# Keys as weights in a fused attention and cosine FFN kernel: scores with keys on partitions, and no turned exponentials

## The chip, the cores and the metric

The kernel runs on one core of one Trainium2 chip. The metric is the device time of one execution in microseconds, the median of several runs. The engines are TensorE (PE; its weight loads are shown apart as PEld), VectorE (DVE), ScalarE (ACT), GpSimd (POOL) and SyncE (SP), which issues the DMA transfers.

## The reference

```python
B, N, C = 4, 12480, 128;  n_agents = 49;  d_ff = 2048      # w_in, w_out float64, the rest float32
def sm(a, b):
    s = (a @ b.transpose(0, 2, 1)) / np.sqrt(128)
    s = s - s.max(-1, keepdims=True)
    e = np.exp(s)
    return e / (e.sum(-1, keepdims=True) + 1e-09)
agent_v = sm(agents, k) @ v        # 49 agents look at 12480 keys
x = (sm(q, agents) @ agent_v).reshape(B * N, 128)
h = x @ w_in                       # 49920 tokens, 2048 columns
out = (h * np.cos(h)) @ w_out
```

## The kernel before

**Main loop.** Each of the 4 batches has 13 groups of 960 queries, 52 groups q in all. A group takes 16 steps, two column halves c of 480 by eight steps i of 256 columns of d_ff, so there are 832 steps n. A step makes the first product on TensorE (`first_product`, L1011: two matmuls with the turned, normalized query weights pT as the moving operand, into one of three PSUM buffers `ph`), the cosine of it on ScalarE (L1014), r = (cos - 1) * h, called the cubic part, on VectorE (L1020), and four steps later (LAG) the second product on TensorE (L1036), which gathers in a PSUM buffer `one`; at the last step of a half two more matmuls (L1032, L1033) add what the -1 took away. `a` is agent_v times w_in, so that x is never made.

**Query weights.** For a group of queries TensorE makes scores (`query_scores`, L169: 32 matmuls with 30 queries as weights and 49 columns each, on four column tiles of TensorE), ScalarE or VectorE copies them to `e`, VectorE takes the maximum (L636), GpSimd subtracts it (L638; `query_both` makes two groups at once, L693), ScalarE takes exponentials of a piece of up to seven groups in one instruction (`query_exp`, L700), GpSimd sums (`query_sum`: additions in a tree, L711, and three small ones, L713 to L715) and, ten steps before the group is used, multiplies by the inverse (L724). `query_turned`, seven steps before, transposes on TensorE (L733), copies to `p` on ScalarE (L737), and on GpSimd makes for each half c a cast of one half of the rows of pT and a subtraction for the other (L740, L741). There are three pT buffers, q % 3; `first_product` of group q reads them.

**Keys of batches 1 to 3** (class `Later`; batch 0 is `First`, ahead of the loop). The work for batch b is done while the loop is at batch b - 1, whose 208 steps are one period. `scores` (13 groups of 1024 keys): two matmuls of 512 columns with the agents as weights, one into rows 0 to 63 and one into rows 64 to 112 of a buffer `one` (L524, L526), so that agents lie on partitions and keys in columns; ScalarE copies to `s` (L531), VectorE takes the maximum of the 512 (L532). `top` makes of these the shift of each agent. The first three groups of batch 1 are scored ahead of the rest, in a short window of their own near the start of the loop (`early_fill`). Then, 97 steps into the period, comes the burst: ScalarE loads its table of exponentials and takes, one after the other, seven groups of queries (A), all keys (L536, 113 x 6240, with the bias of the shift and a sum into `accum_out`) and the other six groups of queries (B). After it `turn` brings keys to partitions (four transposes L544, a copy L548 to `et`), and `values` multiplies them with the values (32 matmuls on four column tiles, L491) and adds to `av` on VectorE (L563). At the period's end `folded`, `inverse` (L501 to L503), `project` and `project_out` make the next batch's `a` and `b1`, `b2`.

**Order.** `Plan` lists, by step, the side work that is written between the loop's instructions; `extra` takes the next free step, `spread_out` spreads a list up to a step, `fill` puts side work into the five steps behind a burst, `mixed` merges two lists. The instructions are then ordered by a scheduler for each engine, by readiness. Fixed against it are what `keep_in_program_order` and `behind` name, the seven steps of a burst on TensorE, VectorE and ScalarE (`as_traced(queues[:3])`, so not GpSimd), side work on VectorE (`kept_behind`) and the late sums of piece B on GpSimd. Loads on SP are held 24 steps back (`load`). Everything else on GpSimd stands where the scheduler puts it, and each engine works through its queue in order.

## Time and profile before

| what | value |
|---|---|
| median of 3 runs | 1119.84 us (1119.44 to 1119.99) |
| the profiled execution: time, its span | 1121.91 us, 1120.1 us |
| mean granted clock of TensorE | 0.979 of full speed |
| TensorE busy | 1060.6 us (95%) |
| VectorE busy | 1028.8 us (92%) |
| ScalarE busy | 980.5 us (88%) |
| GpSimd busy | 373.2 us (33%) |
| chain that ended last | TensorE 62%, VectorE 25%, ScalarE 7% |

The shares are means over the whole span. The three bursts (near 230, 490 and 760 us) and the two stages around each of them, key scores before and values after, have limits of their own, and are read stretch by stretch. A row of the groups gives instructions of one line with their busy time, the mean of one, and the idle time of the engine before them with what ended most of it.

### The profile page before, as it was taken

How to read it: one execution, taken by the hardware profiler on the slowest of the kernel's cores; microseconds unless marked ns; L12 is line 12 of the kernel's file. 1: busy time of each engine (PE TensorE's matmuls, PEld its weight loads, DVE VectorE, ACT ScalarE, POOL GpSimd, SP SyncE). 2: the span in 40 equal slices, each digit the busy share in tenths (PEclk: the TensorE clock that was granted, in tenths of full speed). 3: DMA queues.
4: the chain of work that ended last, by engine and by line, in shares of the span. 5: the costliest groups of instructions: out<-in, count | busy, mean ns of one | idle time of the engine just before them, and what ended most of it. 6: DMA issues, size and time to landing. Idle time of an engine off the chain costs nothing.

```text
span 1120.1 us, 26308 instructions
## 1 busy us (share of the span) xinstructions
PE 1060.6 (95%) x10719; PEld 795.0 (71%) x10719; DVE 1028.8 (92%) x1156; ACT 980.5 (88%) x1275; POOL 373.2 (33%) x658
## 2 busy tenths in 40 slices
PE   6779999799999999989999999979999999989997
PEld 2666677588876776768887777658887777767774
DVE  5749999699999999989998999989999999999997
ACT  4758988888889999998888999999998999999996
POOL 2012322583222313286313232258331323162320
PEclk9889999899999999989999999989999999999999
DMA  9734445523102233434111233441300000000001
GB/s 360 268 129 129 129 145 202 184 94 110 61 19 85 72 120 127 149 128 131 59 56 37 75 107 111 150 147 57 106 28 19 36 18 36 36 18 36 18 36 38
DMA packets 32545, 108.31 MB, mean 97 GB/s; under 512 B 3616, under 2 KB 4896, under 8 KB 32416
## 3 DMA queue, kind: packets, MB, share of 16 engines
q1 hardware_dynamic: 32416, 106.55, 28.2%
q8 instruction: 86, 1.41, 0.5%
q14 instruction: 43, 0.35, 0.1%
HBM read 80.97 MB, written 25.56 MB: 95 GB/s over the span
## 4 chain that ended last, share of the span: by engine, by line
PE 62%; DVE 25%; ACT 7%; issue 3%; DMA 2%; SPq 0%; POOL 0%; ACTq 0%; DVEq 0%
PE ph L1011 24%; DVE r L1020 22%; PE one L1036 22%; ACT c L1014 3%; PE one L491 3%; PE one L169 2%; PE one L544 2%; ACT s L536 1%; PE one L1032 1%; PE one L1033 1%; DMA c<-qT 1%; PE one L733 1%; PE ph L491 1%; PE one L524 1%; PE one L374 1%
## 5 line engine op out<-in xcount | busy, mean ns | idle before, releaser
L1020 DVE SCALAR_TENSOR_TENSOR r<-c,ph 128x960 fp32r<-128x960 f32 x832 | 910.8, 1148 | 36.7 <-ACT c L1014 33.5
L1014 ACT ACTIVATE c<-ph 128x960 f32<-128x960 f32 x832 | 791.1, 980 | 88.0 <-PE ph L1011 66.4
L1011 PE MATMUL ph<-pT,a 113*128 113x480 f32 x1664 | 536.1, 402 | 10.3 <-DVE r L1020 7.2
L1036 PE MATMUL one<-r,w 128*128 128x480 f32 x1664 | 512.6, 391 | 2.6 <-ACT osb L1043 0.9
L1011 PEld LDWEIGHTS ph<-pT,a 113*128 113x128 f32 x1664 | 295.2, 190 | 137.6 <-DVE r L1020 77.3
L1036 PEld LDWEIGHTS one<-r,w 128*128 128x128 f32 x1664 | 309.4, 190 | 62.0 <-issue 8.1
L724 POOL TENSOR_TENSOR p<-e,rz 126x392 f32<-126x392 f32 x51 | 43.1, 846 | 288.3 <-PE one L733 265.4
L741 POOL TENSOR_TENSOR pT<-p,pT 49x480 fp32r<-49x480 f32 x102 | 124.4, 1219 | 7.8
L638 POOL TENSOR_TENSOR e<-e,mx 126x392 f32<-126x392 f32 x43 | 36.3, 844 | 231.5 <-DVE mx L636 231.5
L740 POOL CAST pT<-p 49x480 fp32r<-49x480 f32 x102 | 59.4, 583 | 83.8 <-ACT p L737 79.4
L1043 ACT COPY osb<-one 128x480 f32<-128x480 f32 x80 | 44.8, 560 | 2.3 <-PE one L1036 2.2
L169 PEld LDWEIGHTS one<-ag,xt 128*32 128x32 f32 (+1 forms) x2752 | 33.1, 109 | 17.9 <-issue 14.5
L711 POOL TENSOR_TENSOR tree<-tree 126x96 f32<-126x96 f32 x132 | 39.9, 302 | 9.9
L169 PE MATMUL one<-ag,xt 128*32 128x49 f32 (+1 forms) x2752 | 39.4, 209 | 3.0 <-issue 2.8
L524 PE MATMUL one<-xt,agp 128*64 128x512 f32 (+1 forms) x78 | 39.7, 591 | 1.7 <-DVE tops L528 1.7
L1032 PE MATMUL one<-pT,b 113*128 113x480 f32 x104 | 40.6, 391 | 0.0
L1033 PE MATMUL one<-pT,b 113*128 113x480 f32 x104 | 40.1, 386 | 0.0
L526 PE MATMUL one<-xt,agp 128*49 128x512 f32 (+1 forms) x78 | 39.2, 585 | 0.0
L491 PEld LDWEIGHTS one<-et,vt 128*32 128x32 f32 (+1 forms) x2352 | 28.4, 109 | 13.3 <-issue 11.0
L544 PE MATMUL one<-ident,s 113*128 113x113 f32 (+1 forms) x147 | 23.4, 284 | 13.5 <-ACT s L536 11.3
L491 PE MATMUL one<-et,vt 128*32 128x49 f32 (+1 forms) x2352 | 33.8, 208 | 0.0
L733 PEld LDWEIGHTS one<-ident,p 126*113 126x113 f32 x204 | 28.7, 176 | 4.4 <-POOL tree L711 0.5
(148 smaller groups left out, 670.5 us busy)
## 6 DMA issues: line engine op xcount, KB each, us to landing
outT<-osb SPq DMA_DIRECT2D x51, 480.0 KB, 2.6
xt<-qT SPq DMA_DIRECT2D x49, 480.0 KB, 3.7
xt<-kT SPq DMA_DIRECT2D x43, 512.0 KB, 3.7
vt<-vk SPq DMA_DIRECT2D x42, 512.0 KB, 4.3
c<-kT SPq DMA_DIRECT2D x5, 512.0 KB, 7.6
vt<-w_in SPq DMA_DIRECT2D x8, 256.0 KB, 7.7
vt<-w_out SPq DMA_DIRECT2D x8, 256.0 KB, 7.8
c<-vk SPq DMA_DIRECT2D x3, 512.0 KB, 7.8
```

Source lines behind the costliest of these rows:

```text
L169: mm = nc.tensor.matmul(out[at:at + n], xt[:, t * TT + lo:t * TT + lo + n], ag, start=True, stop=True)
L491: mm = nc.tensor.matmul(po[rows], vt[:, h * k + t, rows], e[:, t, h * HI:h * HI + NA], start=(first and t == h == 0), stop=(last and t == ...
L524: mm = nc.tensor.matmul(ps[:HI], agp[:, self.b], xt[:, :n], start=True, stop=True)
L544: mm = nc.tensor.transpose(pt[:, t], part[:, t * w:(t + 1) * w], ident[:KR, :KR])
L740: nc.gpsimd.tensor_copy(pT[own, c], p[own])
L741: nc.gpsimd.tensor_sub(pT[other, c], p[own], pT[own, c].bitcast(F32))
L1011: nc.tensor.matmul(ph[:, j, :CH], ai[:, f], pTs[q % 3][:, c], start=True, stop=True)
L1014: nc.scalar.activation(cos, h, AF.Sin, bias=HALF_PI, scale=1.0)
L1020: nc.vector.scalar_tensor_tensor(r, cos, 1.0, h, op0=ALU.subtract, op1=ALU.mult)
L1032: nc.tensor.matmul(po, b1[k], pTs[q % 3][:, c], start=False, stop=False)
L1033: nc.tensor.matmul(po, b2[k], pTs[q % 3][:, c], start=False, stop=False)
L1036: nc.tensor.matmul(po, w1[:, f, :], r[:, j, :], start=(f == 0), stop=(f == NF - 1))
```

## The change

For batches 1 to 3 the keys become the weights of their own scores: 32 matmuls on four column tiles for 1024 keys, as for queries, so that `s` is [128 keys, 98, 49 agents] and keys lie on partitions at once. The last group is 2 tiles of 96 keys; the empty rows are set to -1e30. Per group VectorE keeps a running maximum of 392 columns (`run`) where it reduced 512. `top`, `across` and `spread` (a reduction, a transpose with a reduction, a matmul that brings the maximum to all partitions) stand 22 steps before the burst, and 13 subtractions on GpSimd (`shift`) follow them, one a step; three groups of queries are scored after them. The exponential of the keys is one instruction of 4802 columns without bias and sum. The sum comes from 12 additions on GpSimd (`add`), planned 47 steps after the burst's start and every third step from there, and from a reduction, a copy and a matmul with ones at the period's end (`total`, `inverse`). `turn` is gone; `values` reads `s` itself, and the burst's third step gets two of them in the place of two turns.

```diff
@@ -404,6 +404,8 @@

     FULL = 2 * 4 * P
     NL = -(-N // FULL)
+    REST = (N - (NL - 1) * FULL) // 2
+    NT_K = 8 * (NL - 1) + 2
...
@@ -481,17 +484,15 @@
             self.av = self.sb.tile([P, KR], F32, name="av", bufs=2)
             nc.gpsimd.memset(self.av[:, NA:HI], 0.0)

-        def weighted(self, po, e, vt, first, last):
-
-            _, k, _ = e.shape
-            for t in range(k):
-                for h in range(2):
-                    for j in range(P // QS):
-                        rows = slice(j * QS, (j + 1) * QS)
-                        mm = nc.tensor.matmul(po[rows], vt[:, h * k + t, rows], e[:, t, h * HI:h * HI + NA],
-                                              start=(first and t == h == 0), stop=(last and t == k - 1 and h == 1))
-                        if t == h == j == 0:
-                            behind(mm)
+        def weighted(self, po, es, vt, first, last):
+
+            for x, e in enumerate(es):
+                for j in range(P // QS):
+                    rows = slice(j * QS, (j + 1) * QS)
+                    mm = nc.tensor.matmul(po[rows], vt[:, x, rows], e,
+                                          start=(first and x == 0), stop=(last and x + 1 == len(es)))
+                    if x == j == 0:
+                        behind(mm)
...
     class Later(First):

-
-
         def scores(self, g, by_vector=False):
             sb = self.sb
             if g == 0:
-                self.s = sb.tile([KR, N // 2], F32, name="s", bufs=1)
-                self.tops = sb.tile([KR, NL], F32, name="tops", bufs=1)
-                self.zs = sb.tile([KR, 1], F32, name="zs2", bufs=1)
-                self.turned = {}
-                self.m, self.z = (sb.tile([KR, 2], F32, name=x, bufs=1) for x in ("m", "z"))
-                for x in (self.m, self.z):
-                    nc.gpsimd.memset(x, 0.0)
+                self.s = sb.tile([P, NT_K, NA], F32, name="s", bufs=1)
+                self.run = sb.tile([P, 8, NA], F32, name="run", bufs=1)
+                self.es = sb.tile([P, 8, NA], F32, name="es", bufs=1)
+                nc.gpsimd.memset(self.s[REST:, 8 * (NL - 1):], -1e30)
             n = min(FULL, N - g * FULL)
             xt = sb.tile([P, 2 * 512], F32, name="xt", bufs=3)[:, :n]
             load(xt, kT[self.b, :, g * FULL:g * FULL + n])
-            n //= 2
-            ps = self.psum()[:KR, :n]
-            mm = nc.tensor.matmul(ps[:HI], agp[:, self.b], xt[:, :n], start=True, stop=True)
-            behind(mm)
-            nc.tensor.matmul(ps[HI:KR], agp[:, self.b, :NA], xt[:, n:], start=True, stop=True)
-            if by_vector:
-                nc.vector.tensor_tensor_reduce(self.part(g), ps, zero.to_broadcast([KR, n]), 1.0, LOWEST, op0=ALU.add,
-                                               op1=ALU.max, accum_out=self.tops[:, g:g + 1])
-            else:
-                nc.scalar.copy(self.part(g), ps)
-                nc.vector.reduce_max(self.tops[:, g:g + 1], ps, axis=AX.X)
-
-        def exp(self, g, n):
-            e = self.s[:, g * FULL // 2:min((g + n) * FULL, N) // 2]
-            return nc.scalar.activation(e, e, AF.Exp, bias=self.shift, scale=SC, accum_out=self.zs[:, :1])
-
-        def turn(self, g, by_vector=False):
-            part = self.part(g)
-            n = part.shape[-1]
-            k, w = -(-n // P), min(n, P)
-            pt = self.psum()[:w, :k * KR].rearrange("p (t a) -> p t a", a=KR)
+            s = self.part(g)
+            w, k, _ = s.shape
+            ps = self.psum()[:w, :k * NA].rearrange("p (t a) -> p t a", a=NA)
             for t in range(k):
-                mm = nc.tensor.transpose(pt[:, t], part[:, t * w:(t + 1) * w], ident[:KR, :KR])
-                if t == 0:
-                    behind(mm)
-            e = self.sb.tile([P, CH], F32, name="et", bufs=3)[:w, :k * KR].rearrange("p (t a) -> p t a", a=KR)
-            (nc.vector.tensor_copy if by_vector else nc.scalar.copy)(e, pt)
-            self.turned[g] = e
+                for j in range(w // QS):
+                    mm = nc.tensor.matmul(ps[j * QS:(j + 1) * QS, t], xt[:, t * w + j * QS:t * w + (j + 1) * QS],
+                                          ag[:, self.b, :], start=True, stop=True)
+                    if t == j == 0:
+                        behind(mm)
+            (nc.vector.tensor_copy if by_vector else nc.scalar.copy)(s, ps)
+            if g > 0:
+                run = self.run[:w, :k]
+                nc.vector.tensor_max(run, self.part(0) if g == 1 else run, s if by_vector else ps)
+
+        def part(self, g):
+            return self.s[:, 8 * g:8 * g + 8] if g + 1 < NL else self.s[:REST, 8 * g:]
+
+        def top(self):
+            self.m = self.sb.tile([P, NA], F32, name="m", bufs=1)
+            nc.vector.tensor_reduce(self.m, self.run.rearrange("p t a -> p a t"), axis=AX.X, op=ALU.max)
+
+        def across(self):
+            pt = self.psum()
+            nc.tensor.transpose(pt[:NA, :P], self.m, ident)
+            mx = self.sb.tile([NA, 1], F32, name="mx", bufs=1)
+            nc.vector.reduce_max(mx, pt[:NA, :P], axis=AX.X)
+            self.mxw = self.sb.tile([NA, P], F32, name="mxw", bufs=1)
+            nc.vector.tensor_copy(self.mxw, mx.to_broadcast([NA, P]))
+
+        def spread(self):
+            pb = self.psum()
+            nc.tensor.matmul(pb[:, :NA], self.mxw, ident[:NA, :NA], start=True, stop=True)
+            self.mxb = self.sb.tile([P, NA], F32, name="mxb", bufs=1)
+            nc.vector.tensor_copy(self.mxb, pb[:, :NA])
+
+        def shift(self, g):
+            s = self.s[:, 8 * g:min(8 * g + 8, NT_K)]
+            nc.gpsimd.tensor_sub(s, s, self.mxb.unsqueeze(1).to_broadcast(list(s.shape)))
+
+        def exp(self):
+            return nc.scalar.activation(self.s, self.s, AF.Exp, scale=SC)
+
+        def add(self, g):
+            s = self.s[:, 8 * g:min(8 * g + 8, NT_K)]
+            es = self.es[:, :s.shape[1]]
+            nc.gpsimd.tensor_add(es, self.s[:, :8] if g == 1 else es, s)

         def values(self, g):
-            e = self.turned.pop(g)
+            e = self.part(g)
             w, k, _ = e.shape
-            vt = self.sb.tile([P, 2 * 4, P], F32, name="vt", bufs=VT).rearrange("p t d -> p (t d)")
-            vt = vt[:w, :2 * k * P].rearrange("p (t d) -> p t d", d=P)
+            vt = self.sb.tile([P, 2 * 4, P], F32, name="vt", bufs=VT)[:w, :k]
             load(vt, vk[self.b, g] if g + 1 < NL else vk_rest[self.b])
             po = self.psum()[:, :NA]
-            self.weighted(po, e, vt, True, True)
+            self.weighted(po, [e[:, t] for t in range(k)], vt, True, True)
             if g == 0:
                 self.clear()
                 nc.vector.tensor_copy(self.av[:, :NA], po)
             else:
                 nc.vector.tensor_add(self.av[:, :NA], self.av[:, :NA], po)
+
+        def total(self):
+            self.es2 = self.sb.tile([P, KR], F32, name="es2", bufs=1)
+            nc.gpsimd.memset(self.es2[:, NA:HI], 0.0)
+            nc.vector.tensor_reduce(self.es2[:, :NA], self.es.rearrange("p t a -> p a t"), axis=AX.X, op=ALU.add)
+            nc.vector.tensor_copy(self.es2[:, HI:], self.es2[:, :NA])
+
+        def inverse(self):
+            self.total()
+            pa = self.psum()
+            nc.tensor.matmul(pa[:KR, :1], self.es2, ones, start=True, stop=True)
+            self.rz = self.sb.tile([KR, 1], F32, name="rz", bufs=1)
+            nc.vector.tensor_scalar_add(self.rz, pa[:KR, :1], EPS)
+            nc.vector.reciprocal(self.rz, self.rz)
...
-        def fill(at, queries, turns, values):
+        def fill(at, queries, values):

             taken.update(range(at, at + 5))
-            for i, work in enumerate(('q', 'D', 'qtt', '', '')):
+            for i, work in enumerate(('q', 'D', 'qvv', '', '')):
                 on = early_plan if 0 < i < 4 else plan
                 for x in work:
                     if x == "D" and len(queries) > 1:
                         on(at + i, query_both, *queries.pop(0)[1:3])
                         queries.pop(0)
                     else:
-                        todo = dict(q=queries, D=queries, t=turns, v=values)[x]
+                        todo = dict(q=queries, D=queries, v=values)[x]
                         if todo:
-                            f, *args = todo.pop(0)
-                            on(at + i, list, in_parts(f, *args, *(True,) * (x == "t")))
+                            on(at + i, list, in_parts(*todo.pop(0)))
                 if 2 <= i < 4:
                     on(at + i, summed, at, 9)

@@ -945,30 +971,31 @@

         later = []
         ahead = 0
+        AFTER, TURN = 3, 22
         for b in range(1, NB):
             o, ps = (b - 1) * PER, pieces[b - 1]
             at = o + BURST
             qs = [x for piece in ps for x in scored(piece)][ahead:]
             ks = [(ab[b].scores, g) for g in range(3 if b == 1 else 0, NG)]
-            t = spread_out(mixed(ks, qs), t, at - 8, b == 1 or True)
-            t = extra(t, ab[b].top, dense=True)
+            before = sum(1 for x in qs) - AFTER
+            t = spread_out(mixed(ks, qs[:before]), t, at - TURN, True)
+            t = extra(t, ab[b].across, dense=True)
+            plan(t - 1, ab[b].top)
+            t = extra(t + 1, ab[b].spread, dense=True) + 1
+            for g in range(NL):
+                plan(t + g, ab[b].shift, g)
+            t = spread_out(qs[before:], t, at - 5, True)
             assert t < at, (t, at)
-            work = dict(A=(query_exp, ps[0]), B=(query_exp, ps[1]), K=(pinned_exp, ab[b], 0, NG))
+            work = dict(A=(query_exp, ps[0]), B=(query_exp, ps[1]), K=(pinned_exp, ab[b]))
             burst(at, [work[x] for x in ('A', 'K', 'B')])
             fresh = scored(pieces[b][0], False, True)
             ahead = len(fresh)
-            turns, vs = [(ab[b].turn, g) for g in range(NG)], [(ab[b].values, g) for g in range(NG)]
+            vs = [(ab[b].values, g) for g in range(NG)]
             judged(at)
-            fill(at, fresh, turns, vs)
+            fill(at, fresh, vs)
             fresh = [x[:3] for x in fresh]
-            done = NG - len(turns)
-            rest, vs = vs, []
-            if not turns[0][1] - rest[0][1]:
-                vs.append(turns.pop(0))
-            while rest:
-                if turns and turns[0][1] - rest[0][1] < 2:
-                    vs.append(turns.pop(0))
-                vs.append(rest.pop(0))
+            for g in range(1, NL):
+                plan(at + 44 + 3 * g, ab[b].add, g)
             t, end = at + 5, o + PER - 26
             todo = mixed(vs, fresh)
```

Three places in the order of the engines' queues; xN after a row counts like rows.

GpSimd in the burst of batch 2, from the end of the fifth query sum of piece A (`rz`, `tree`) to the first cast of the next group's pT, before:

```order
L715 TENSOR_TENSOR rz_2941<-rz_2941,e 126x8
L711 TENSOR_TENSOR tree<-e 126x192
L711 TENSOR_TENSOR tree<-tree 126x8x12
L711 TENSOR_TENSOR tree<-tree 126x8x6
L711 TENSOR_TENSOR tree<-tree 126x8x3
L713 TENSOR_TENSOR rz_2941<-tree 126x8
L714 TENSOR_TENSOR rz_2941<-rz_2941,tree 126x8
L715 TENSOR_TENSOR rz_2941<-rz_2941,e 126x8
L740 CAST pT_100<-p 49x480 x2
L741 TENSOR_TENSOR pT_100<-p,pT_100 49x480 x2
```

and after, with the end of the sixth query sum:

```order
L563 TENSOR_TENSOR es<-es,s 128x392
L741 TENSOR_TENSOR rz_3322<-rz_3322,tree 126x8
L563 TENSOR_TENSOR es<-es,s 128x98
L742 TENSOR_TENSOR rz_3322<-rz_3322,e 126x8
L738 TENSOR_TENSOR tree<-e 126x192
L738 TENSOR_TENSOR tree<-tree 126x8x12
L738 TENSOR_TENSOR tree<-tree 126x8x6
L738 TENSOR_TENSOR tree<-tree 126x8x3
L740 TENSOR_TENSOR rz_3322<-tree 126x8
L741 TENSOR_TENSOR rz_3322<-rz_3322,tree 126x8
L742 TENSOR_TENSOR rz_3322<-rz_3322,e 126x8
L767 CAST pT_100<-p 49x480 x2
```

The additions of the keys' exponentials (L563, `es`), twelve of them, stand interleaved with the fourth to sixth query sums, ahead of the casts (now L767) of pT.

GpSimd ahead of that burst, where the last pT before it is made (`pT_99`), before:

```order
L740 CAST pT_98<-p 49x480 x2
L741 TENSOR_TENSOR pT_98<-p,pT_98 49x480 x2
L638 TENSOR_TENSOR e<-e,mx_6148 126x392
L740 CAST pT_99<-p 49x480 x2
L741 TENSOR_TENSOR pT_99<-p,pT_99 49x480 x2
L518 MEMSET m 113x2
L638 TENSOR_TENSOR e<-e,mx_6388 126x392
```

and after:

```order
L767 CAST pT_98<-p 49x480 x2
L768 TENSOR_TENSOR pT_98<-p,pT_98 49x480 x2
L555 TENSOR_TENSOR s<-s,mxb 128x392 x5
L665 TENSOR_TENSOR e<-e,mx_6763 126x392
L555 TENSOR_TENSOR s<-s,mxb 128x392 x7
L555 TENSOR_TENSOR s<-s,mxb 128x98
L665 TENSOR_TENSOR e<-e,mx_6858 126x392
L767 CAST pT_99<-p 49x480 x2
L768 TENSOR_TENSOR pT_99<-p,pT_99 49x480 x2
```

All 13 subtractions of the keys' maximum (L555) and two of queries now stand between the two pT.

TensorE in the burst of batch 2, ahead of the first product (L1011) of the next group of queries, before:

```order
L169 MATMUL one<-ag,xt 30x49
L544 MATMUL one<-ident,s 128x113 x8
L1032 MATMUL one<-pT_98,b_95 128x480
L1033 MATMUL one<-pT_98,b_97 128x480
L1036 MATMUL one<-r,w_78 128x480 x2
L1011 MATMUL ph<-pT_99,a_93 128x480 x2
```

and after:

```order
L169 MATMUL one<-ag,xt 30x49
L492 MATMUL one<-s,vt 32x49 x64
L1059 MATMUL one<-pT_98,b_95 128x480
L1060 MATMUL one<-pT_98,b_97 128x480
L1063 MATMUL one<-r,w_78 128x480 x2
L1038 MATMUL ph<-pT_99,a_93 128x480 x2
```

Two groups of values (L492) take the place of two turns (L544); the products around them stand as before.

## Rows read from the trace of the kernel before

**Rows 1.** Busy times by stretch: us, PE, PEld, DVE, ACT, POOL busy, PEclk, DMA, GB/s

```profile
351.70:462.00 110.30, 109.38 (x837) 79.30 (x825) 108.10 (x109) 101.28 (x125) 28.48 (x33) 1.00 0.38 122
462.00:498.60 36.60, 30.36 (x433) 23.67 (x434) 31.04 (x42) 33.66 (x33) 22.94 (x61) 0.86 0.39 125
498.60:595.30 96.70, 96.29 (x1315) 79.83 (x1316) 92.51 (x102) 84.59 (x109) 40.33 (x74) 1.00 0.22 71
887.00:983.00 96.00, 95.37 (x405) 69.39 (x403) 95.83 (x91) 91.11 (x117) 25.14 (x29) 1.00 0.08 31
```

**Rows 2.** Chain of waits, long pieces: start us, us, what

```profile
887.52 98.79 DVE r L1020 x92
```

**Rows 3.** Timeline of GpSimd, burst of batch 2: start us, us, what, shapes, count

```profile
487.11 0.60 POOL L711 TENSOR_TENSOR tree<-e 126x192 f32<-126x192 f32 x1
...
487.67 1.65 POOL L693 TENSOR_TENSOR e<-e,mx 126x392 f32<-126x392 f32 x2
...
491.82 0.60 POOL L711 TENSOR_TENSOR tree<-e 126x192 f32<-126x192 f32 x1
...
494.39 0.60 POOL L711 TENSOR_TENSOR tree<-e 126x192 f32<-126x192 f32 x1
...
496.92 1.23 POOL L740 CAST pT<-p 49x480 fp32r<-49x480 f32 x2
498.22 2.51 POOL L741 TENSOR_TENSOR pT<-p,pT 49x480 fp32r<-49x480 f32 x2
```

**Rows 4.** Timeline of TensorE behind that burst, 498 to 503 us

```profile
498.52 0.90 PE L169 MATMUL one<-ag,xt 128*32 128x49 f32 x64
...
499.35 0.49 PE L1036 MATMUL one<-r,w 128*128 128x480 f32 x1
...
500.98 0.55 PE L544 MATMUL one<-ident,s 113*128 113x113 f32 x4
...
501.30 0.68 PE L1036 MATMUL one<-r,w 128*128 128x480 f32 x2
...
501.82 0.60 PE L1011 MATMUL ph<-pT,a 113*128 113x480 f32 x2
```

**Rows 5.** Timelines of GpSimd and TensorE, bursts of batches 1 and 3

```profile
233.47 2.51 POOL L741 TENSOR_TENSOR pT<-p,pT 49x480 fp32r<-49x480 f32 x2
...
236.44 0.60 PE L1011 MATMUL ph<-pT,a 113*128 113x480 f32 x2
...
763.66 2.52 POOL L741 TENSOR_TENSOR pT<-p,pT 49x480 fp32r<-49x480 f32 x2
...
767.21 0.61 PE L1011 MATMUL ph<-pT,a 113*128 113x480 f32 x2
```

**Rows 6.** Timeline of TensorE at a group of key scores

```profile
457.36 0.64 PE L524 MATMUL one<-xt,agp 128*64 128x512 f32 x1
...
458.36 0.70 PE L1011 MATMUL ph<-pT,a 113*128 113x480 f32 x2
```

**Rows 7.** Groups by line: engine, what, count | busy us, mean ns | idle before

```profile
L741 POOL TENSOR_TENSOR pT<-p,pT 49x480 fp32r<-49x480 f32 x102 | 124.4, 1219 | 7.8
L711 POOL TENSOR_TENSOR tree<-e 126x192 f32<-126x192 f32 x44 | 26.6, 604 | 8.6 <-ACT e L700 8.4
L636 DVE TENSOR_REDUCE mx<-e 126x8 f32<-126x392 f32 x43 | 23.9, 555 | 2.3 <-ACT e L632 1.7
L532 DVE TENSOR_REDUCE tops<-one 113x1 f32<-113x512 f32 x33 | 22.5, 681 | 0.0
L536 ACT ACTIVATE s<-s,mx 113x6240 f32<-113x6240 f32 x3 | 16.4, 5481 | 0.0
```

**Rows 8.** Busy times by stretch behind the wait for the exponentials, columns as Rows 1

```profile
485.00:490.00 5.00, 5.00 (x15) 3.97 (x14) 4.16 (x6) 4.65 (x6) 4.45 (x12) 0.55 0.24 98
490.00:495.00 5.00, 5.00 (x86) 4.29 (x85) 4.16 (x6) 3.93 (x6) 4.29 (x14) 1.00 0.40 110
```

More of the change, by code (lines that the diff above doesn't have):

```diff
@@ L475, in values @@
                 self.clear()
-            self.weighted(self.po, e, vt, g == 0, g == NL - 1)
+            self.weighted(self.po, [e[:, t, h * HI:h * HI + NA] for h in range(2) for t in range(k)], vt,
+                          g == 0, g == NL - 1)
             if g == NL - 1:
@@ L741, in query_turned, with pinned_exp @@
                 nc.gpsimd.tensor_sub(pT[other, c], p[own], pT[own, c].bitcast(F32))
-        def pinned_exp(ab, g, n):
-            tc.keep_in_program_order(ab.exp(g, n))
+        def pinned_exp(ab):
+            tc.keep_in_program_order(ab.exp())
         def sine_table():
@@ L991, in agent_attention_cos_ffn @@
         judged(at)
-        fill(at, [], [], [])
+        fill(at, [], [])
         def pinned_largest(c):
```

## The prediction

> **What bounds the kernel now.** I read the busy times by stage first, for batch 2: 351.7 to 462 us is the stage in which its key scores are made, 462 to 498.6 the burst of exponentials, 498.6 to 595.3 the stage of values, and 887 to 983 a stretch with no key work at all. See in [rows 1] that three engines are near their limit together. In the score stage VectorE is busy 108.10 of 110.30 us; in the value stage TensorE is busy 96.29 of 96.70 and VectorE still 92.51. In the stretch without key work VectorE is busy 95.83 of 96.00, and the chain of waits there is one row, 92 cubic parts of 128x960 in 98.79 us, 1.074 us each [rows 2]. So a batch cannot go below VectorE's own work, and what TensorE gives up is worth at most VectorE's idle time: 2.2 us per score stage and 4.2 us per value stage. The burst is different: in its 36.6 us TensorE is busy 30.36 and VectorE 31.04, since ScalarE makes exponentials instead of cosines.
>
> Then I looked at what GpSimd does between the burst and the next group of queries, and when TensorE first reads that group's weights pT. That decides this forecast. In the burst of batch 2 GpSimd goes straight through seven query sums, three subtractions, two casts and two subtractions for pT; the first of those last two ends at 498.22 + 1.22 = 499.44 [rows 3], and TensorE's first product from that pT starts at 501.82 [rows 4]. The slack is 2.4 us. In the other two bursts it is 236.44 - 234.69 = 1.7 and 767.21 - 764.88 = 2.3 us [rows 5]. The profile shows no wait of a product for GpSimd's pT, but only by these 2 us.
>
> **The change, part by part.** *Scores.* The keys become the weights. A group of 1024 keys holds TensorE from 457.36 to 458.36 now, 1.00 us [rows 6]; query scores are already made in the new form, 32 matmuls on four column tiles, and take 498.52 to 499.35, 0.83 us [rows 4]. That is 0.17 us less per group, 2 us per batch. On VectorE the reduction of 512 (681 ns) becomes a maximum of 392 elements, for which I take the reduction of 392, 555 ns [rows 7]: 12 x 0.126 = 1.5 us less per batch, of which the new top, its transpose, its spreading and their copies (four operations of 0.2 to 0.55 us, where four of 0.15 stood) take back 0.7. VectorE is the limit there, so I count 1.2 us per batch, between 0 and 3.0 (all its idle time as well).
>
> *Turns.* Eleven of 13 turns lie in the value stage. Each holds TensorE from 500.98 to 501.30, 0.32 us [rows 4], so 3.5 us per batch go; ScalarE's 11 copies go as well, but ScalarE is busy only 84.59 of 96.70 there. TensorE would need 92.8, VectorE needs 92.5. Two engines that are both full do not run without waits: I take 2.0 us of the possible 3.6, and 0 as the lower end.
>
> *Exponential.* One of 4802 columns instead of 6240. At 5481 ns for 6240 [rows 7] that is some 4.2 us and no accumulator to read: 1.3 us shorter. It lets ScalarE's cosines start earlier, but see what is late next.
>
> *GpSimd, shifts.* Thirteen subtractions per batch are new, 12 of 392 columns, ahead of the burst. They stand in its queue ahead of the casts of the last pT before the burst, together with two query subtractions. The nearest rows for 392 columns are 0.71 us (below) and 1.03, so the shifts take 9 to 13 us, and with the two subtractions (1.65) and a cast and subtraction for pT (2.4) that pT is there 13 to 17 us after the maximum is spread; TensorE reads it 13 steps later, 13 x 1.074 and three query scores, 15 to 17 us. Between 0 and 2.4 us of stall per batch; I take 0.7.
>
> *GpSimd, adds.* Twelve additions per batch, 11 of 392 columns and one of 98, replace the accumulator's sum. The plan asks for them 47 steps after the burst and later, but in the order of the built program all twelve stand within the fourth to sixth of the burst's seven query sums, **ahead of the casts of pT**. GpSimd works its queue in order, so pT is late by what they take. No addition of this shape is in the trace. Lower end: three operations of 392 columns put into the fifth sum stretch it from 494.39 - 491.82 = 2.57 to 491.82 - 487.11 = 4.71 us [rows 3], 0.71 each: 11 x 0.71 + 0.2 = 8.0. Those have a broadcast operand. Upper end: the operations with two full operands, 604 ns for 192 columns and 1219 for 480 [rows 7], put 392 at 604 + 200 x 615/288 = 1031 ns: 11 x 1.03 + 0.4 = 11.7. An addition has two full operands, so I start from 11.7; but the three in the fifth sum took 0.34 less than three times the 0.825 of their own (two in 1.65), since they stand at two places between dependent operations and fill a gap at each, 0.17 us. With 11 places that is 1.8 to 1.9: **9.9 us**.
>
> So TensorE stands before its first product from that pT, and everything behind it in its queue, second products too, stands with it; the three buffers of first products run dry and ScalarE and VectorE stop. Per burst 9.9 less the slack: 7.5, 8.2 and 7.6 us, together **23.3 us** (17.6 to 28.7). The stall ends when GpSimd lets it, so whatever TensorE and ScalarE save inside the burst, the shorter exponential above all, is swallowed by it.
>
> The Trainium skill (GPSIMD Engine Reference, 4.1 Engine selection) speaks against this placing: it advises VectorE for an elementwise addition and calls GpSimd about twice slower; its section 3.1 gives about 2.6 cycles an element at 1.2 GHz, from which 0.85 us for 392 is an estimate. By it the three stalls would be some 17 us and the sum near 1134.
>
> *After the stall.* Behind TensorE's wait for the exponential the granted clock is 0.55 from 485 to 490 us, most of it at 1.2 GHz, and 1.00 from 490 on [rows 8]. Behind a wait of 7 us I expect the lower level again. Five microseconds at 0.55 are 2.25 us of TensorE's work not done; part of that falls into the wait itself. I take 1.2 us per burst (0 to 2.3).
>
> *Sum of the weights.* A reduction and a copy on VectorE stand before the matmul of the total instead of two short reductions: 0.4 us per batch.
>
> **The sum.** The profiled execution took 1121.9 us, its span is 1120.1, and the median of the runs is 1119.84, 0.2% below the profiled one; the difference is added to the median. Stalls +23.3, colder clock +3.6, late casts before the burst +2.1, totals +1.2, value stages -6.0, score stages -3.6: **+20.6, 1140 us**. Apart from batch 1's first three groups of keys, the stretches up to 119 us and from 887 us on hold none of the changed work.
>
> The Trainium skill (TensorEngine Tiling (Array Packing), PSUM Bottleneck) says that tiling speeds the matmuls up but not the emptying of PSUM. The busy times of the score stage agree, VectorE 108.10 of 110.30 us; with no gain at all in the score stages the sum would be 1144.
>
> **Rivals.** (1) *The queue does not matter, and the kernel gets faster.* If the twelve additions delayed pT by less than the 2 us of slack, GpSimd would never be waited for; value stages -6.0, score stages -3.6, 1.0 per burst from the shorter exponential and totals +1.2 give 1119.8 - 11.4 = 1108. For it: GpSimd is idle most of the value stage, 40.33 of 96.70 busy [rows 1], and its present queue keeps nobody waiting. Against: each addition would have to cost under 0.2 us, and the shortest 392-column row is 0.71. It decides from 2 us of delay on. (2) *Nothing to see.* The lower end of the additions, 17.6 us of stall, all of VectorE's idle time won (value stages -10.8, score stages -8) and no cold clock: 1119 us. (3) *Both queues are late.* The shifts cost 1.03 each and hold the casts before the burst by 2.4 us too, each stall with its cold clock: 23.3 + 7.2 + 7.2 + 1.2 - 9.6 = +29, 1149 us.
>
> **How the numbers follow.** Forecast 0.66, rival 1 0.09, rival 2 0.08, rival 3 0.17. The order of GpSimd's queue is fixed, so I give the stall itself 0.85 and more; its size is what is open. The range leaves out rival 1, a part of rival 2 and what lies beyond rival 3: 1121 to 1153. A difference of 0.2% is about what runs of this kernel can tell from none. Faster by more than that 0.09, within it 0.08, slower 0.83.
>
> **What would show it.** Right: three idle times of TensorE of 6 to 9 us before a first product, put down to GpSimd's pT, about 24 us after the start of each burst's first exponential; twelve additions of 0.8 to 1.1 us ahead of that cast; a granted clock at half behind it; then value stages 1 to 3 us shorter. Wrong: no such wait, or pT ready before TensorE comes; or additions that run where the plan has them.

## The result and the profile after

The changed kernel takes 1136.03 us (median of 4 runs, 1132.91 to 1137.56), the kernel before beside it 1119.76: ratio 1.0142, 95% interval 1.0118 to 1.0166. It is slower by 16.3 us; 20.6 was forecast, 1140 us.

The busy times of the three stages of batch 2 and of the stretch without key work, which answer to [rows 1] (same columns):

```profile
346.00:458.00 112.00, 111.13 (x1526) 87.63 (x1526) 109.72 (x115) 101.31 (x130) 32.43 (x37) 1.00 0.39 124
458.00:509.10 51.10, 37.51 (x696) 29.77 (x696) 38.70 (x46) 38.37 (x40) 45.02 (x85) 0.86 0.37 124
509.10:603.00 93.90, 93.03 (x1083) 73.74 (x1083) 88.69 (x96) 80.88 (x97) 40.28 (x74) 0.98 0.16 57
887.00:983.00 96.00, 95.19 (x403) 69.44 (x402) 95.59 (x90) 90.70 (x115) 25.50 (x29) 1.00 0.07 26
```

The stages on either side are as full as before, the value stage a little shorter. In the stretch of the burst TensorE is busy 37.51 of 51.10 us, and GpSimd 45.02: the idle engine has become the busiest. GpSimd's own timeline there, which answers to [rows 3] (start, length, what, count):

```profile
488.22 1.04 POOL L563 TENSOR_TENSOR es<-s 128x392 f32<-128x392 f32 x1
...
491.10 1.03 POOL L563 TENSOR_TENSOR es<-es,s 128x392 f32<-128x392 f32 x1
492.09 0.28 POOL L738 TENSOR_TENSOR tree<-tree 126x48 f32<-126x48 f32 x1
492.34 1.04 POOL L563 TENSOR_TENSOR es<-es,s 128x392 f32<-128x392 f32 x1
...
503.54 0.41 POOL L563 TENSOR_TENSOR es<-es,s 128x98 f32<-128x98 f32 x1
...
506.60 1.22 POOL L767 CAST pT<-p 49x480 fp32r<-49x480 f32 x2
507.90 2.47 POOL L768 TENSOR_TENSOR pT<-p,pT 49x480 fp32r<-49x480 f32 x2
```

All twelve additions run ahead of the casts, 1.04 us each, with steps of the query sums between them. TensorE in the same stretch, which answers to [rows 4] (in brackets the idle time before, and what ended it), and below it the waits of the whole span (engine, line, what it waited for: us in total, times, longest):

```profile
498.91 0.60 PE L1063 MATMUL one<-r,w 128*128 128x480 f32 x2
509.14 1.17 PE L1038 MATMUL ph<-pT,a 113*128 113x480 f32 x2 [9.63 <-POOL pT L768]
```

```profile
PE ph L1038 <- POOL pT L768: 29.2, 5, 9.6
```

TensorE stands 9.63 us until GpSimd's first subtraction for pT is done at 507.90 + 1.2. The five waits of the last row are one in each burst, 8.45, 9.63 and 9.64 us, and two of 0.7 us ahead of the bursts of batches 2 and 3. In the profile before, no such row exists. The chain that ended last now goes through GpSimd, where it had 0%:

```profile
PE 46%; DVE 30%; POOL 12%; ACT 7%; issue 4%; DMA 0%; SPq 0%; ACTq 0%; POOLq 0%; DVEq 0%
```

The groups of the new operations (line engine op, shapes, count | busy us, mean ns | idle before):

```profile
L558 ACT ACTIVATE s<-s 128x4802 f32<-128x4802 f32 x3 | 12.6, 4191 | 0.0
L530 DVE TENSOR_TENSOR run<-run,one 128x392 f32<-128x392 f32 x29 | 16.1, 554 | 0.0
L537 DVE TENSOR_REDUCE m<-run 128x49 f32<-128x392 f32 x3 | 2.5, 841 | 0.0
L555 POOL TENSOR_TENSOR s<-s,mxb 128x392 f32<-128x392 f32 x36 | 33.3, 969 | 17.1 <-DVE mxb L551 17.1
L563 POOL TENSOR_TENSOR es<-es,s 128x392 f32<-128x392 f32 x30 | 31.2, 1039 | 0.0
```

The first product of each group of queries can be counted off in both traces, and where its start moves against the other trace is where time goes. After minus before, by the start's shift over each stretch, batches 1, 2, 3:

| stretch | forecast | measured |
|---|---|---|
| key scores up to the burst | -1.2 + 0.7 | -0.9, -1.0, -1.0 |
| burst, to the first product from the next pT | +8.2, +7.5, +7.6 | +8.1, +6.9, +7.0 |
| the group behind it | +1.2 | +0.5, +0.5, +0.6 |
| values and totals | -2.0 + 0.4 | -2.2, -2.1, -2.1 |
| the last burst, without keys | 0 | +1.1 |
| sum from the first step to the last | +20.6 | +15.2 |

Ahead of the loop the two profiled executions differ by 4.1 us (first step at 72.1 and 68.0 us), in a part that the change does not touch; in all the traces below it starts at 68.2 to 71.8. Single executions of one kernel scatter by as much, so that stretches are compared within the loop. One version below was traced twice: its two traces differ by 1.2 us in the key scores of batch 1, by 0.4 in its burst and by 0.6 in the last burst, and by 0.1 or less in the other rows of this table.

### The profile page after: what moved, and what is told of

Same layout as the page of the kernel before. It is cut to its first block, busy times and chain, and to the rows that moved or that the text cites. A ratio compares the mean times of both kernels' runs of the same rounds, so it can differ in the third digit from the quotient of the medians.

```text
span 1131.0 us, 30442 instructions
## 1 busy us (share of the span) xinstructions
PE 1047.6 (93%) x12759; PEld 800.4 (71%) x12759; DVE 1021.0 (90%) x1144; ACT 958.5 (85%) x1239; POOL 440.0 (39%) x733
## 4 chain that ended last, share of the span: by engine, by line
PE 46%; DVE 30%; POOL 12%; ACT 7%; issue 4%; DMA 0%; SPq 0%; ACTq 0%; POOLq 0%; DVEq 0%
DVE r L1047 26%; PE ph L1038 19%; PE one L1063 16%; ACT c L1041 4%; POOL s L555 3%; POOL es L563 3%; POOL tree L738 3%; PE one L492 2%; PE one L523 1%; PE one L169 1%; PE one L1059 1%; PE one L1060 1%; PE ph L492 1%; PE one L760 1%; ACT e L727 1%
## 5 line engine op out<-in xcount | busy, mean ns | idle before, releaser
L1063 PE MATMUL one<-r,w 128*128 128x480 f32 x1664 | 505.3, 390 | 0.9 <-issue 0.5
L1038 PEld LDWEIGHTS ph<-pT,a 113*128 113x128 f32 x1664 | 288.4, 190 | 167.5 <-DVE r L1047 75.2
L767 POOL CAST pT<-p 49x480 fp32r<-49x480 f32 x102 | 59.4, 582 | 61.9 <-ACT p L764 57.1
L492 PEld LDWEIGHTS one<-s,vt 128*32 128x32 f32 (+1 forms) x2352 | 31.8, 117 | 20.3 <-issue 11.1
L169 PEld LDWEIGHTS one<-ag,xt 128*32 128x32 f32 x2752 | 33.5, 110 | 16.8 <-issue 15.1
L492 PE MATMUL one<-s,vt 128*32 128x49 f32 (+1 forms) x2352 | 37.8, 218 | 8.0 <-ACT s L558 6.8
L169 PE MATMUL one<-ag,xt 128*32 128x49 f32 x2752 | 39.7, 210 | 2.3 <-issue 2.3
L555 POOL TENSOR_TENSOR s<-s,mxb 128x392 f32<-128x392 f32 (+1 forms) x39 | 34.4, 927 | 17.1 <-DVE mxb L551 17.1
L523 PEld LDWEIGHTS one<-ag,xt 128*32 128x32 f32 x2340 | 28.4, 110 | 15.2 <-issue 7.7
L523 PE MATMUL one<-ag,xt 128*32 128x49 f32 x2340 | 33.8, 209 | 1.9 <-DVE s L527 1.9
L563 POOL TENSOR_TENSOR es<-es,s 128x392 f32<-128x392 f32 (+1 forms) x33 | 32.4, 982 | 0.0
```

The costliest lines, as they stand in the source:

```text
L169: mm = nc.tensor.matmul(out[at:at + n], xt[:, t * TT + lo:t * TT + lo + n], ag, start=True, stop=True)
L492: mm = nc.tensor.matmul(po[rows], vt[:, x, rows], e, start=(first and x == 0), stop=(last and x + 1 == len(es)))
L523: mm = nc.tensor.matmul(ps[j * QS:(j + 1) * QS, t], xt[:, t * w + j * QS:t * w + (j + 1) * QS], ag[:, self.b, :], start=True, stop=True)
L555: nc.gpsimd.tensor_sub(s, s, self.mxb.unsqueeze(1).to_broadcast(list(s.shape)))
L563: nc.gpsimd.tensor_add(es, self.s[:, :8] if g == 1 else es, s)
L767: nc.gpsimd.tensor_copy(pT[own, c], p[own])
```

## The experiments

The theory is that TensorE waits because twelve additions stand ahead of the casts in GpSimd's queue. The rivals are that the additional work costs time wherever it stands, or that the new layout does. "Loop" is the time from the first product of step 0 to that of step 831 in each trace: before 1037.6, after 1052.8 us.

**The additions behind the casts.**

```diff
+        def lazy_add(x, g):
+            with kept_behind([nc.gpsimd.engine]):
+                x.add(g)
...
-                plan(at + 44 + 3 * g, ab[b].add, g)
+                plan(at + 44 + 3 * g, lazy_add, ab[b], g)
```

> The changed kernel with its twelve additions per batch held on GpSimd behind what is written before them in their planned steps, so that they stand behind the casts of the next group's pT. Queue theory (TensorE waits because the additions stand ahead of these casts): the three waits of TensorE for GpSimd's pT, 9.6 us each, go; pT is then ready about when TensorE comes, so 0 to 0.5 us of each stays, and 1.5 us of colder clock goes too: 1136 - 27 to - 29, 1107 to 1109 us. Rival, work theory (GpSimd's additional work, wherever it stands, or the new layout itself costs the time): 1133 to 1137 us, with the waits found at later pT.

1105.3 us, ratio to before 0.987 (0.9853 to 0.9886); loop 1019.5. The same additions, the same layout, and 31 us less than after. GpSimd and TensorE in the burst of batch 2:

```profile
488.72 1.22 POOL L767 CAST pT<-p 49x480 fp32r<-49x480 f32 x2
490.02 2.52 POOL L768 TENSOR_TENSOR pT<-p,pT 49x480 fp32r<-49x480 f32 x2
```

```profile
490.78 0.60 PE L1067 MATMUL one<-r,w 128*128 128x480 f32 x2
491.30 0.70 PE L1042 MATMUL ph<-pT,a 113*128 113x480 f32 x2
```

The casts follow the last query sum at once. TensorE starts 0.06 us behind the end of the first subtraction (490.02 + 1.22) and has stood 0.1 us at most: pT comes just when TensorE does, and the slack of before is used up. Behind the burst the granted clock is full, where it was down in the changed kernel (first row after, second row here; columns as [rows 1]):

```profile
509.10:514.10 5.00, 4.96 (x16) 4.22 (x17) 1.67 (x2) 2.16 (x3) 4.39 (x10) 0.69 0.00 0
491.30:496.30 5.00, 5.00 (x24) 4.34 (x24) 4.95 (x6) 4.25 (x6) 4.43 (x10) 1.00 0.16 63
```

Against after, each burst is shorter by 9.7 us and the group behind it by 1.3 to 1.4; every other stretch moves by 0.1 us or less up to the last burst, but for 0.7 us near the loop's start. The position is the whole loss. It gave more than expected, since 1.3 to 1.4 us of colder clock goes in each burst and not 0.5, and this version beats both kernels.

**Six subtractions of the maximum behind the last casts ahead of the burst, too.**

```diff
+        def lazy_shift(x, g):
+            with kept_behind([nc.gpsimd.engine]):
+                x.shift(g)
...
             for g in range(NL):
-                plan(t + g, ab[b].shift, g)
+                if g < 7:
+                    plan(t + g, ab[b].shift, g)
+                else:
+                    plan(at - 7 + (g - 7) // 2, lazy_shift, ab[b], g)
```

> As e1, and six of the thirteen subtractions of the maximum held behind the casts of the last pT before the burst. Queue theory: the 2.1 us that batches 2 and 3 each lose ahead of the burst go, 3 to 5 us less than e1: 1103 to 1106 us. Rival: the subtractions come too late for the keys' exponential, which then waits for GpSimd 1 us or more behind the first exponential: no gain over e1, or 1 to 6 us more.

1104.51 us, ratio 0.9866 (0.9848 to 0.9884), not to be told from the one above. Its expectation was wrong in size. In the changed kernel TensorE's wait ahead of the burst is one row:

```profile
470.36 0.70 PE L1038 MATMUL ph<-pT,a 113*128 113x480 f32 x2 [0.71 <-POOL pT L768]
```

So 0.7 us of the 2.1 that batches 2 and 3 lose there is GpSimd's; with the subtractions moved 0.9 goes, and 0.6 and 1.1 come back in the bursts of batches 2 and 3. The rest, 1.3 us, stays, and beside it stand the new maximum (L537, 841 ns) and the three short operations behind it on VectorE; that these are its cause was not tried apart.

**The additions on VectorE.**

```diff
-            nc.gpsimd.tensor_add(es, self.s[:, :8] if g == 1 else es, s)
+            nc.vector.tensor_add(es, self.s[:, :8] if g == 1 else es, s)
```

> The changed kernel with its twelve additions per batch on VectorE, at the planned steps. The three waits for GpSimd's pT go, as in e1 (to 1107 to 1109). Twelve additions of about 0.55 us, 6.6 us per batch, fall on an engine that is busy 88.7 of 93.9 us in the value stage. Theory that VectorE's work is the limit there: 4 to 6 us per batch come back, 1120 to 1127 us. Rival, that VectorE has room for them between its waits: 1108 to 1112 us.

1113.93 us, ratio 0.9941 (0.9925 to 0.9958), between the two ranges expected; the waits in the bursts are gone, and 3.9 to 4.4 us per value stage, the lower end of what VectorE as the limit would cost, are lost against the version with the additions behind the casts. (The medians of the two lie 8.6 us apart, the traced executions 13.7.) Busy times over the same four groups of queries in that version, and here:

```profile
509.50:583.70 74.20, 73.46 (x882) 57.87 (x881) 72.44 (x78) 65.14 (x79) 35.89 (x50) 1.00 0.15 54
```

```profile
514.50:592.60 78.10, 76.09 (x883) 56.99 (x882) 77.58 (x90) 65.87 (x79) 24.69 (x38) 1.00 0.14 51
```

VectorE was busy 72.44 of 74.20 and has no room: of its 5.1 us more, 3.9 lengthen the stage. One addition takes 599 ns there:

```profile
L563 DVE TENSOR_TENSOR es<-es,s 128x392 f32<-128x392 f32 x30 | 18.0, 599 | 0.0
```

The Trainium skill (GPSIMD Engine Reference, 4.1 Engine selection) advises VectorE for this operation. Its ratio of about two is nearly borne out, 1039 against 599 ns, 1.7; its choice is not, since the slower engine has the time to spare here.

**No additions at all.**

```diff
             for g in range(1, NL):
-                plan(at + 44 + 3 * g, ab[b].add, g)
+                pass
...
-            nc.vector.tensor_reduce(self.es2[:, :NA], self.es.rearrange("p t a -> p a t"), axis=AX.X, op=ALU.add)
+            nc.vector.tensor_reduce(self.es2[:, :NA], self.s[:, :8].rearrange("p t a -> p a t"), axis=AX.X, op=ALU.add)
```

> The changed kernel without the twelve additions per batch; the total is taken from the first eight tiles of exponentials alone, so the sum of the weights is left out in part. Queue theory: as e1 within 1 us, 1107 to 1109 us, since where they are behind the casts the additions cost nothing. Rival: clearly below e1, by 3 us or more, if GpSimd's additions cost time in the value stage too.

8433 us: with so small a sum the projected weights exceed a bound of the kernel (FAST_MAX), and the program does all groups over again on its general path, which fills the trace from 1110 us on. The loop itself can still be read, and takes 1019.3 us against 1019.5 with the additions behind the casts (1020.5 in a second trace of these). There they cost nothing that can be seen.

**The kernel before, with twelve such additions and nothing else.**

```diff
+        def add(self, g):
+            if g == 1:
+                self.es = self.sb.tile([KR, 392], F32, name="es", bufs=1)
+            part = self.s[:, g * 392:(g + 1) * 392]
+            nc.gpsimd.tensor_add(self.es, self.s[:, :392] if g == 1 else self.es, part)
...
+            for g in range(1, 13):
+                plan(at + 44 + 3 * g, ab[b].add, g)
```

> The kernel before with nothing changed but twelve additions per batch on GpSimd, 113 x 392, planned at the steps of the changed kernel; their result is used by nobody. They stand, as there, ahead of the casts of the next group's pT. Queue theory: pT 9.3 to 9.8 us later, less the 1.8 to 2.4 us of slack, makes TensorE wait 7 to 8 us per burst, and a colder clock behind it costs 0.5 to 1.4: 23 to 27 us more than before, 1142 to 1147 us. Rival, the new layout costs the time and not the additions: 1119 to 1122 us.

1153.41 us, ratio 1.0296 (1.0272 to 1.032), more than either theory gave; loop 1068.5, 30.9 more than before. The old layout with the additions shows the same wait:

```profile
PE ph L1019 <- POOL pT L747: 25.2, 3, 8.8
```

The bursts grow by 8.6, 8.0 and 8.0 us, at and above the upper end of what was expected: twelve additions of full width delay the casts by 10.3 us, and not by 9.3 to 9.8. The rest is the group behind each, +2.8, +1.4 and +2.3, where 0.5 to 1.4 was expected. The first 8 us behind each of the three waits (columns as [rows 1]):

```profile
244.39:252.39 8.00, 8.00 (x84) 6.46 (x85) 3.80 (x6) 3.77 (x5) 6.88 (x18) 0.62 0.23 68
520.53:528.53 8.00, 8.00 (x90) 6.43 (x91) 4.91 (x7) 5.04 (x6) 6.88 (x18) 0.81 0.18 66
795.22:803.22 8.00, 8.00 (x29) 6.80 (x30) 3.87 (x5) 4.70 (x7) 6.88 (x18) 0.70 0.01 2
```

TensorE is busy throughout, and the lower the clock, the more the group behind has grown.

**The kernel before, with two.** The same edit with `range(1, 3)`.

> The kernel before with two such additions per batch instead of twelve. Queue theory with its slack: pT comes 1.7 to 2.1 us later, TensorE had 1.8, 2.4 and 2.3 us: no wait, or 0.3 us in one burst, 1119 to 1121 us. Rival, each addition costs its share of the time, whatever the slack: a sixth of the twelve's, 4 us, 1124 us.

1120.99 us, ratio 1.0007 (0.9996 to 1.0017). The bursts move by 0.0, -0.3 and -0.5 us; the casts come 1.7 us later, and one wait for pT, 0.3 us in batch 3, is in the trace. Two additions fit into the slack, twelve do not: delay costs only beyond the slack, as rival 1 said, and the change lies far beyond it.

**Four of the twelve behind the casts, eight ahead.**

```diff
-                plan(at + 44 + 3 * g, ab[b].add, g)
+                plan(at + 44 + 3 * g, *((ab[b].add, g) if g < 7 else (lazy_add, ab[b], g)))
```

> The changed kernel with the last four of the twelve additions behind the casts and eight still ahead. Queue theory: pT comes 2.9 to 3.5 us earlier than with twelve, the wait falls from 9.6 to 6.1 to 6.7 us, the colder clock behind it stays: 9 to 10 us less than 1136, 1126 to 1128 us. Rival, a wait has one price whatever its length: 1133 to 1137 us.

1125.85 us, ratio 1.0053 (1.0037 to 1.007). The longest wait is 6.9 us, and that of batch 2 is 6.43 where it was 9.63:

```profile
506.37 1.17 PE L1042 MATMUL ph<-pT,a 113*128 113x480 f32 x2 [6.43 <-POOL pT L768]
```

In the other two bursts it is 6.85 where it was 8.45, and 6.88 where it was 9.64. So the wait has no fixed price: four additions fewer ahead of the casts take 1.6 to 3.2 us off it.

**Turns put back.** In the version with the additions behind the casts, eleven turns per batch as unused work.

```diff
+        def turn(self, g):
...
+                mm = nc.tensor.transpose(pt[:, t], flat[:KR, lo:lo + P], ident[:KR, :KR])
...
+            nc.scalar.copy(et, pt)
...
+            vs = [x for v in vs for x in ((ab[b].turn, v[1]), v)]
             todo = mixed(vs, fresh)
```

> The kernel with its additions behind the casts (1105 us) and, as work that nobody uses, eleven turns per batch put back into the value stage: four transposes of 113 x 128 on TensorE and a copy on ScalarE each. The prediction's term (2.0 us per value stage): 1110 to 1112 us. Theory that TensorE alone is the limit of this stage: 11 x 0.32 us and more, 1115 to 1118 us. Theory that VectorE alone is: 1105 to 1106 us.

1112.15 us, ratio 0.9933 (0.9907 to 0.9959); loop 1029.1, 9.6 more, 3.2 per batch. By the medians it is 2.3 per batch against the first runs of the version without turns, and 3.1 against its second (1102.84 us, below), so that the median alone lies at the range of the prediction's term. By the traces its 2.0 was too low, and TensorE's whole 3.5 is nearer. TensorE is busy 75.85 of 76.20 us over the four groups of batch 2, VectorE 72.84:

```profile
514.60:590.80 76.20, 75.85 (x913) 61.68 (x911) 72.84 (x79) 66.99 (x86) 34.77 (x48) 1.00 0.18 63
```

**A longer exponential, in the changed kernel and in the one with the additions behind the casts.**

```diff
             tc.keep_in_program_order(ab.exp())
+            more = sb.tile([P, 29, NA], F32, name="more", bufs=1)
+            tc.keep_in_program_order(nc.scalar.activation(more, ab.s[:, :29], AF.Exp, scale=SC))
```

> The changed kernel with the keys' exponential made longer again: a second instruction of 1421 columns behind it on ScalarE, 1.2 to 1.4 us, whose result nobody uses. Theory that the wait for GpSimd ends the burst and swallows what ScalarE saves or loses in it: no change, 1134 to 1137 us, and waits of TensorE for pT shorter by 1.2 to 1.4 us each. Rival, the exponential's length counts in full: 1.3 us per burst, 1139 to 1141 us.

1134.97 us, ratio 1.0132 (1.0115 to 1.0149), against 1.0142 without it. Each burst moves by 0.1 us, and the wait shrinks:

```profile
PE ph L1040 <- POOL pT L768: 26.5, 5, 8.3
```

The longest was 9.6 us: in batches 2 and 3 the wait is 1.3 us shorter, so ScalarE's added work, 1.4 us, lies wholly within the wait for GpSimd. In batch 1 it shrinks by 0.2 only (8.45 to 8.29), and why TensorE did not come later there was not looked into. (The groups behind the bursts of batches 2 and 3 are 2.1 us longer in this trace, at a lower clock; the last section has it.)

> The kernel with the additions behind the casts (1105 us) and the same longer exponential. Same theory: without the wait for GpSimd the length counts, 1.2 to 1.4 us per burst, 1108 to 1110 us. Rival, TensorE or GpSimd hides it there too: 1104 to 1106 us.

1104.49 us, against 1105.3 on another chip: the medians show nothing. The traces do; each of the three bursts is 1.3 us longer, all else within 0.1 from the first burst to the last, and the instruction takes

```profile
L773 ACT ACTIVATE more<-s 128x1421 f32<-128x1421 f32 x3 | 4.2, 1391 | 0.1
```

To settle this, both ran again, side by side.

> The kernel with the additions behind the casts again, beside the one with the longer exponential on the same chip, since the medians of the two (1105.3 and 1104.5 us, on different chips) don't show the 1.3 us per burst that their traces show. If the traces tell the truth: 3 to 4 us less than the other one, both within 1103 to 1109 us.

> The one with the longer exponential again: 3 to 4 us more than the one beside it. Rival: what the length costs in the burst is lost in what varies between executions, and the medians agree within 1 us.

1102.84 (ratio 0.9848, 0.9825 to 0.987) and 1106.43 us (0.9875, 0.9854 to 0.9897): 3.6 us apart, though the two intervals overlap; in their traces the three bursts differ by 0.9, 1.3 and 1.3 us. The same microsecond of ScalarE counts or not by what ends the burst.

## Why the prediction was right, and where its sizes were off

**The reading that decided it held.** The slack of 1.7 to 2.4 us, read off the end of one GpSimd row and the start of one TensorE row [rows 3 to 5], and twelve additions ahead of the casts in the queue, give a wait; the bursts grew by 8.1, 6.9 and 7.0 us where 8.2, 7.5 and 7.6 were forecast. The delay of the casts, counted from the start of the burst's first exponential, was 9.7 to 9.8 us in all three, forecast 9.9. One addition took 1.04 us, the upper bound worked out from rows with two full operands [rows 7]; the discount for gaps that they fill was right and a little small, 2.1 us where 1.8 to 1.9 was taken. The estimate of 0.85 us, worked out from the Trainium skill (GPSIMD Engine Reference, 3.1 Elementwise), was too low.

**The shorter exponential was swallowed**, as forecast (4191 ns where 5481 stood, 1.3 us), and the runs with a longer one show it. For the same reason the three idle times, 8.45, 9.63 and 9.64 us, are longer than the growth of the bursts, and two of them longer than the 6 to 9 us that the prediction gave as a sign: TensorE reaches the wait earlier than it reached that product before.

**Late casts ahead of the burst**: 0.7 us forecast for each batch; 0.71 and 0.75 in batches 2 and 3, none in batch 1. The 0.7 was picked from a range of 0 to 2.4, so that it fits is luck.

**Key scores** gained 3.1 us over the first five groups of queries of batches 2 and 3 and lost 2.1 in the sixth, where the maxima are joined and spread and TensorE waits; 1.0 remains (0.9 in batch 1), where 0.5 was counted. VectorE is as full as before, 109.72 of 112.00 us.

**The colder clock was sized about right.** Forecast 1.2 us per burst; against the version without the wait it is 1.3 to 1.4. The 0.5 to 0.6 of the table hold a gain as well: in the version without the wait the same group of queries is 0.8 to 0.9 us shorter than before, as part of the turns' work is gone there.

**The turns were the largest term off**: 2.0 us against 3.2. The step that failed is the one that took two full engines to share the gain; with 73.00 us of VectorE and 76.26 of TensorE over the four groups before, TensorE was the later one:

```profile
521.00:597.70 76.70, 76.26 (x980) 62.56 (x976) 73.00 (x81) 66.70 (x87) 22.02 (x32) 1.00 0.21 69
```

**Rival 1 was right about everything but the queue**, and too modest: it put the kernel without the wait at 1108, and it runs in 1103 to 1105. There the bursts are 7.2 us shorter than before in all, where it counted 3.0, and the groups behind them with the value stages 9.2, where it counted 4.8.

**Why 1136 and not 1140.** Over the three batches, key scores with the late casts gave -2.8 us (forecast -1.5), the bursts +22.0 (+23.3), and the groups behind them with the values and totals -5.0 (-1.2); the last burst, forecast at nothing, cost +1.1. Single executions of one kernel differ by about as much as the forecast was off, so the nearness of the total says less than the terms do.

Rival 3 can be excluded by the 0.71 and 0.75, where it needs 2.4 in each batch. Rival 2 had waits too, and is excluded by their size: an addition took 1.04 us, not 0.71, the bursts grew by 22.0 us, not 17.6, and the clock did fall. (As its terms are printed, rival 2 adds up to 1120; its 1119 comes out with 9 us for the score stages, three times the 3.0 named above it.)

## What to carry to other kernels

An engine that is busy a third of the time can still be the one that is waited for: what counts is the slack between the row that makes a buffer ready and the row that reads it, and what a scheduler puts ahead of it in the same queue. Off-path work should be pinned behind the urgent work, not only planned late; here that turned 1.4% slower into 1.3 to 1.5% faster without changing an operation. And savings ahead of such a wait should not be counted until the wait is gone.

## What was not expected of the hardware

The last burst holds no key work, and its instructions and the wait ahead of them (3.81 us) are the same in both traces; yet it is 1.1 us longer after. The rows of before, and of after shifted by 10 us (columns as [rows 1]), show that the granted clock differs from the second row on:

```profile
995.00:997.00 2.00, 2.00 (x6) 1.65 (x7) 1.87 (x3) 1.44 (x3) 1.65 (x6) 0.50 0.00 0
997.00:1000.00 3.00, 3.00 (x13) 2.48 (x12) 2.49 (x3) 2.46 (x4) 2.45 (x9) 0.81 0.13 54
1000.00:1002.00 2.00, 2.00 (x13) 1.78 (x12) 2.00 (x3) 2.00 (x4) 1.61 (x7) 1.00 0.41 165
```

```profile
1005.00:1007.00 2.00, 2.00 (x6) 1.65 (x7) 1.87 (x3) 1.46 (x3) 1.63 (x6) 0.50 0.00 0
1007.00:1010.00 3.00, 3.00 (x9) 2.52 (x8) 2.27 (x2) 2.06 (x3) 2.45 (x9) 0.50 0.13 51
1010.00:1012.00 2.00, 2.00 (x11) 1.73 (x11) 1.41 (x2) 1.39 (x3) 1.61 (x7) 0.86 0.41 169
```

Behind the same wait and with the same work the clock stayed at 0.50 (1.2 GHz) for two more microseconds in one execution. One kernel shows it by itself: in the two traces of the version with the additions behind the casts, the same eleven steps from the first product behind that wait took 13.35 and 12.68 us (13.77 after, 12.71 before). What a wait costs in clock therefore differs from one execution to another. Behind the waits for pT, in nine of them (three each in the changed kernel, in it with the longer exponential and in the old layout with twelve additions), the group behind was 1.3 to 1.5 us longer than without the wait where the granted clock of the first 8 us was 0.81, 2.2 to 2.3 at 0.69 or 0.70, and 2.6 to 2.8 at 0.61 or 0.62.
